# Attention scores as 64x64 products on the four quarters of the TensorE array, under a plan with other priorities

## Chip, cores and metric

One core of one Trainium2 chip. The metric is the device time of one execution in microseconds (us); lower is better. The kernel is one program: five engines, each with its own instruction queue in a fixed order, which wait for each other by semaphores.

## What is computed

Linear attention with decay in blocks, then two MLPs, all in float32. Cut to what matters here:

```python
# q, k, v: batch 2, 8 heads, 768 tokens, 64 wide
for b in range(nb):                                  # blocks of 64 tokens
    intra = einsum('bhic,bhjc->bhij', qb, kb) * Dmask   # scores, masked with lam ** (i - j)
    intra = einsum('bhij,bhjd->bhid', intra, vb)
    inter = einsum('bhid,bhde->bhie', qb * lam_pow, kv_state)
    out[:, :, sl] = intra + inter
    kv_state = lam_block * kv_state + einsum('bhsd,bhse->bhde', kb * rev_pow, vb)
x = heads side by side, (1536, 512)
h = x @ w_in;  x = (h * tanh(softplus(h))) @ w_out       # 512 -> 2048 -> 512
h = x @ w2_in; x = max(h, 0) ** 2 @ w2_out
```

## The kernel before

**Tiles and stages.** The kernel works on blocks of 128 tokens, twelve chunks, six per sequence. `attention(j)` (called for j = 0 to 5) records the operations of two chunks: load q and k (`qk`, transposed, so that the 64 columns of two heads lie on the 128 partitions) and k and v (`kv`); the scores `sc` (L514); their product with the mask on DVE, `a` (L371); the product of `a` with v into `xo` (L559, planned as av); q scaled in place on GpSimd (POOL, `qd`, L528) and k scaled in place (POOL, `kd`, L523); the update `sd` of the state, k times v (L540); the product of the scaled q with the state, added into the same `xo` (L568, "carried", planned as in); scaling (`ss`) and addition (`sa`) of the state on ACT, POOL and DVE; and copies of `xo` to SBUF on ACT and DVE (`xr`, `xh`, `xl`). Two MLPs follow. Each of their products is made as three products of rounded high and low parts (`mm3`, L380): `up`, `p`, `b`, `e`, `ua`, `ub` into the hidden layer, `dn`, `q`, `o`, `v` out of it, most of them by a scheme with seven products of blocks instead of eight. The weights come as 64-bit numbers that ACT (`m`, L658) and DVE (`t`, a shift of integers, L663, then a join L670) turn into float32, ACT and DVE then into high and low parts (`wh`, `wl`).

**Scores.** For each of four pairs of heads p and each head e of a pair, one product: 64 partitions (those of the head) of k, 128 columns, stationary, and 128 columns of q moving; the result takes 128 partitions of one bank of PSUM, bank e. Two products that follow each other use the lower and the upper 64 rows of the array. `carried` makes products of 64x64 stationary by 128 moving columns: 64 rows by head e, and 64 partitions of `xo` as output, so the four products that follow each other use the four quarters of the array.

```python
def weighted(p, e):                 # carried: which half of the output's partitions
    c = e if p < 2 else 1 - e
    return slice(c * D, (c + 1) * D)
for p in range(2):
    for e in range(2):
        for h in (p, p + 2):
            r = slice(e * D, (e + 1) * D)
            nc.tensor.matmul(out=o[weighted(h, e), h, n], lhsT=z[r, h], rhs=qd[r, h], ...)
```

**What sets the order.** Nothing above issues an instruction at once. Each call of `op(engine, us, fn, reads, writes, ...)` records an operation with an assumed duration; `Plan.run` then plays all of them by those durations and writes down the order in which each engine takes them, and that order is issued. PE takes its ready operation of lowest `rank` (which follows the order of the program); the others take the ready one that is due first. `Plan.dues` works the due times out backward from PE's, and the table `SOONER` shifts single ones by some microseconds. A DVE operation that only touches SBUF is lengthened in the plan by 0.8 (`SHARED`) of the time in which POOL works beside it. SP's queue issues all loads in planned order; the list `FIRST` fixes its first twelve.

Of the kernel before, what the change touches and what calls it, by code (L numbers as in the profile page):

```python
# [22 lines left out]
D = 64  # L23
# [10 lines left out]
SHARED = 0.8  # L34
# [69 lines left out]
class Op:  # L104
    def __init__(self, eng, us, fn, name, rank, lag, due, spare):
        self.eng, self.us, self.fn, self.name, self.rank = eng, us, fn, name, rank
        self.lag, self.due, self.spare = lag, due, spare
        self.before, self.after, self.vals = {}, {}, {}
        self.late, self.start, self.end = math.inf, None, None
        self.sooner = 0.0  # L110
        self.port = False


class Plan:
# [16 lines left out]
    def op(self, eng, us, fn, reads=(), writes=(), name="", rank=None, lag=None, due=None, spare=0, ahead=None, table=None, port=True):  # L131
# [17 lines left out]
        for v in o.vals:  # L149
            v.left += 1  # L150
        o.port = eng == "DVE" and port and all(v.space == "S" for v in o.vals)
# [163 lines left out]
def attention_mlps(ctx, tc, lam, qk, kv, w_in, w_out, w2_in, w2_out, out):  # L315
# [1102 lines left out]
    rank = 0  # L1418
# [111 lines left out]
```

## Time and profile before

| | before |
|---|---|
| median of three runs (lowest, highest) | 527.87 us (527.04, 529.77) |
| profiled execution: its time, its span | 527.82 us, 525.8 us |
| PE busy | 517.1 us, 98% of the span |
| DVE, ACT, POOL busy | 466.8, 429.3, 32.1 us |
| PE's share of the chain that ended last | 96% |
| DMA | 134.82 MB, 256 GB/s over the span |

The span is the profiled time from the first instruction to the last; the execution's own time holds some 2 us more around it. "Busy" counts the time in which an engine has an instruction under way; the rows of a matmul are passes, and a float32 product that is not split has two passes, so the 8 products of a chunk's scores are 16 rows of 64*128 (rows by columns of the stationary part). The start of the next row, not a row's duration, tells what a group of passes takes, since passes overlap.

### The profile page before, as it was taken

The page shows a single profiled execution, that of the slowest core. Times are in us where ns is not written, and L with a number is a line of the kernel's source. Part 1 is how long each engine was busy: PE and PEld are TensorE (multiplying, and loading weights), DVE is VectorE, ACT ScalarE, POOL GpSimd, SP SyncE. Part 2 cuts the span into 40 slices and gives each one's busy share as a digit, 9 for nine tenths or more (in the row PEclk, how much of TensorE's full clock was granted, in tenths as well). Part 3 has the DMA queues.
Part 4 walks back from the last instruction along what each step waited for, and adds up shares of the span by engine and source line. Part 5 has one row for each costly group of instructions (what it writes and reads, how often), then busy time and mean ns, then how long its engine had stood idle before and what let it go on. Part 6 is the DMA issues. An engine that isn't in the chain of part 4 may idle for free.

```text
span 525.8 us, 9377 instructions
## 1 busy us (share of the span) xinstructions
PE 517.1 (98%) x3686; PEld 464.6 (88%) x3686; DVE 466.8 (89%) x519; ACT 429.3 (82%) x506; POOL 32.1 (6%) x32
## 2 busy tenths in 40 slices
PE   7999999999999999999999999999999999999997
PEld 4898888898988989889888889998999889988996
DVE  6998998998996879998999999998999589995893
ACT  2859769889999999878999889869999689957852
POOL 2656200000000000000000000000000000000000
PEclk9999999999999999999999999999999999999999
DMA  8999812899479984996246897998289963891015
GB/s 300 410 408 347 342 37 84 272 340 407 181 283 364 320 233 129 347 401 246 80 150 240 351 359 258 336 365 267 78 290 359 347 205 123 303 413 43 1 46 195
DMA packets 39357, 134.82 MB, mean 256 GB/s; under 512 B 4242, under 2 KB 7314, under 8 KB 39314
## 3 DMA queue, kind: packets, MB, share of 16 engines
q1 hardware_dynamic: 39312, 134.23, 69.9%
q8 instruction: 29, 0.48, 0.3%
q14 instruction: 14, 0.11, 0.1%
q10 hardware_dynamic: 2, 0.00, 0.0%
HBM read 108.00 MB, written 26.21 MB: 255 GB/s over the span
## 4 chain that ended last, share of the span: by engine, by line
PE 96%; DVE 2%; DMA 1%; issue 0%; SPq 0%; DVEq 0%
PE p L380 17%; PE q L380 14%; PE v L380 11%; PE e L380 10%; PE o L380 10%; PE b L380 8%; PE ua L380 8%; PE ub L380 6%; PE dn L380 4%; PE up L380 2%; PE xo L559 2%; PE sc L514 2%; DMA st<-in_moe_w_in_dram 1%; PE xo L568 1%; PE sd L540 1%; DVE a L371 1%
## 5 line engine op out<-in xcount | busy, mean ns | idle before, releaser
L658 ACT ACTIVATE m<-st 128x512 f32<-128x512 f32 (+1 forms) x66 | 42.4, 671 | 12.1 <-DMA st<-in_moe_w_in_dram 8.2
L670 DVE SCALAR_TENSOR_TENSOR t<-m,t 128x1024 int32<-128x1024 int32 x32 | 39.4, 1250 | 3.9 <-ACT m L658 3.5
L371 DVE TENSOR_TENSOR sl<-s,sh 128x1024 fp32r<-128x1024 f32 x32 | 38.8, 1221 | 3.2 <-ACT sh L368 2.9
L371 DVE TENSOR_TENSOR wl<-t,wh 128x1024 fp32r<-128x1024 f32 x32 | 39.8, 1249 | 0.0
L371 DVE TENSOR_TENSOR el<-D,eh 128x1024 fp32r<-128x1024 f32 x32 | 38.8, 1219 | 0.8 <-ACT eh L368 0.8
L368 ACT ACTIVATE wh<-t 128x1024 fp32r<-128x1024 f32 x32 | 33.4, 1054 | 5.0 <-DVE t L670 4.8
L368 ACT ACTIVATE sh<-s 128x1024 fp32r<-128x1024 f32 x32 | 33.4, 1053 | 1.0 <-DVE s L371 1.0
L368 ACT ACTIVATE eh<-D 128x1024 fp32r<-128x1024 f32 x32 | 33.1, 1053 | 0.9 <-DVE D L371 0.9
L371 DVE TENSOR_TENSOR el<-h,eh 128x1024 fp32r<-128x1024 f32 x24 | 29.2, 1220 | 4.3 <-ACT eh L368 4.3
L663 DVE TENSOR_SCALAR t<-st 128x512 int32<-128x512 int32 (+1 forms) x66 | 27.3, 453 | 1.2 <-DMA st<-in_moe_w_in_dram 1.1
L368 ACT ACTIVATE eh<-h 128x1024 fp32r<-128x1024 f32 x24 | 25.2, 1056 | 0.3
L380 PE MATMUL p<-fl,wh 128*128 128x512 f32 x64 | 25.3, 395 | 0.0
L380 PE MATMUL p<-fh,wl 128*128 128x512 f32 x64 | 25.0, 391 | 0.0
L380 PE MATMUL p<-fh,wh 128*128 128x512 f32 x64 | 24.9, 389 | 0.0
L380 PE MATMUL p<-fl,sh 128*128 128x512 f32 x64 | 24.9, 389 | 0.0
L380 PE MATMUL p<-fh,sl 128*128 128x512 f32 x64 | 24.9, 389 | 0.0
L380 PE MATMUL e<-fl,sh 128*128 128x512 f32 x64 | 24.9, 389 | 0.0
L380 PE MATMUL e<-fh,sl 128*128 128x512 f32 x64 | 24.9, 389 | 0.0
L380 PE MATMUL p<-fh,sh 128*128 128x512 f32 x64 | 24.9, 389 | 0.0
L380 PE MATMUL e<-fh,sh 128*128 128x512 f32 x64 | 24.9, 389 | 0.0
L371 DVE TENSOR_TENSOR D<-h,h 128x1024 f32<-128x1024 f32 x16 | 18.9, 1220 | 2.1 <-ACT h L907 1.5
L368 ACT ACTIVATE ap<-o 128x1024 f32<-128x1024 f32 x18 | 18.4, 1022 | 2.8 <-PE o L380 2.6
(315 smaller groups left out, 1899.8 us busy)
## 6 DMA issues: line engine op xcount, KB each, us to landing
fh<-f SPq DMA_DIRECT2D x35, 512.0 KB, 5.7
fl<-f SPq DMA_DIRECT2D x35, 512.0 KB, 6.7
st<-in_moe_w_out_dram SPq DMA_DIRECT2D x32, 512.0 KB, 6.5
st<-in_moe_w_in_dram SPq DMA_DIRECT2D x26, 512.0 KB, 6.4
f<-fh SPq DMA_DIRECT2D x14, 512.0 KB, 6.0
f<-fl SPq DMA_DIRECT2D x14, 512.0 KB, 7.7
qk<-in_qk_dram SPq DMA_DIRECT2D x12, 512.0 KB, 10.2
kv<-in_kv_dram SPq DMA_DIRECT2D x12, 512.0 KB, 10.2
```

Of the source, the lines that this page charges most:

```text
L368: nc.scalar.activation(out=o, in_=i, func=AF.Copy)
L371: nc.vector.tensor_tensor(out=o, in0=a, in1=b, op=alu)
L380: nc.tensor.matmul(out=out_, lhsT=a, rhs=b, start=start, stop=pieces or (last and i == 2), skip_group_check=not start if pieces else onto)
L514: nc.tensor.matmul(out=o[:, e, p], lhsT=t[r, 1, p], rhs=t[r, 0, p], start=True, stop=True)
L540: nc.tensor.matmul(out=o[e * D : (e + 1) * D, p], lhsT=t[:, p, 1 + e], rhs=t[:, p, 0 if e else 3], start=True, stop=True)
L559: nc.tensor.matmul(out=o[weighted(p, e), p, n], lhsT=v[:, p, 0 if e else 3], rhs=w[:, e, p], start=p % 2 == n == 0, stop=True, skip_group_ ...
L568: nc.tensor.matmul(out=o[weighted(h, e), h, n], lhsT=z[r, h], rhs=qd[r, h], start=False, stop=True, skip_group_check=True)
L658: nc.scalar.activation(out=tl(m)[o, i], in_=tl(st, TB, 2)[r, :, 1].bitcast(F32), func=AF.Prelu, scale=RANGE, alpha=BELOW)
L663: nc.vector.tensor_scalar(out=tl(t)[o, i], in0=tl(st, TB, 2)[r, :, 0], scalar1=29, scalar2=None, op0=ALU.logical_shift_right)
L670: nc.vector.scalar_tensor_tensor(out=tl(t), in0=tl(m).bitcast(I32), scalar=3, in1=tl(t), op0=ALU.logical_shift_left, op1=ALU.bitwise_or)
```

## The change

Three edits. (1) `scores` splits each product by the columns of k: 16 products of 64x64 by 128 instead of 8 of 64x128 by 128; half 0 writes partitions 0 to 63 of the bank, half 1 partitions 64 to 127, so four products that follow each other use the four quarters. The planned durations become 1.6 and 0.88 us instead of 1.7 and 1.04. (2) The planner: the clocks of the engines start at 0.6 us and SP's at 1.1 instead of 0; the shift `t` of the weights gets `port=2`, with which a `t` that starts while POOL works is lengthened by all that POOL still has to do. (3) `SOONER` is another table, with 52 entries instead of 193. No load is changed: the same loads, with the same sizes; those behind the twelfth stand in another order.

```diff
 SOONER = {
-    "zero.1": -9.0, "lam.1": 28.5, "one.1": -1.5, "rate.1": 24.0, "eye.1": 4.5, "mask0.1": 24.0, "mask1.1": -1.5,
...
+    "eye.1": -1.5, "decay.1": 3.0, "qk0.1": -6.0, "kv0.1": 3.0, "kd0.1": 6.0, "kd1.1": 3.0, "ss1.1": 12.0,
...
@@
-        self.port = False
+        self.port = self.locks = False
@@
+        o.locks = port == 2
         o.port = eng == "DVE" and port and all(v.space == "S" for v in o.vals)
@@
-        clock = dict.fromkeys(self.LAG, 0.0)
+        clock = dict.fromkeys(self.LAG, 0.6)
+        clock["SP"] = 1.1
@@
                 if o.port and clock["POOL"] > now:
-                    o.end += SHARED * min(o.us, clock["POOL"] - now)
+                    o.end += clock["POOL"] - now if o.locks else SHARED * min(o.us, clock["POOL"] - now)
@@
                 t, o = tl(q, 2, NP, CH), tl(sc, 2, NP, CH)
                 for p in range(NP):
-                    for e in range(2):
-                        r = slice(e * D, (e + 1) * D)
-                        nc.tensor.matmul(out=o[:, e, p], lhsT=t[r, 1, p], rhs=t[r, 0, p], start=True, stop=True)
-
-            scored = op("PE", 1.7 if c < 2 else 1.04, scores, [(q, "q"), (q, "k")], [(sc, 0)], name=sc.name, rank=rank + n)
+                    for half in range(2):
+                        m = slice(half * D, (half + 1) * D)
+                        for e in range(2):
+                            r = slice(e * D, (e + 1) * D)
+                            nc.tensor.matmul(out=o[m, e, p], lhsT=t[r, 1, p, m], rhs=t[r, 0, p], start=True, stop=True)
+
+            scored = op("PE", 1.6 if c < 2 else 0.88, scores, [(q, "q"), (q, "k")], [(sc, 0)], name=sc.name, rank=rank + n)
@@
-            op("DVE", 0.34 * len(rows()), low, [(st, 0)], [(t, i)], name=f"t{name}{i}", spare=SPARE[1])
+            op("DVE", 0.34 * len(rows()), low, [(st, 0)], [(t, i)], name=f"t{name}{i}", spare=SPARE[1], port=2)
```

The new table moves instructions on every engine. In the rows below the number behind a name is that of its chunk or weight, and the one behind the underscore that of its buffer; xN is a count of products.

First place: PE, in the opening, from the product of chunk 1 with its masked scores (a1) on. Before:

```order
L559 MATMUL xo0_193<-a1_188,kv1_164 64x128 x8
L540 MATMUL sd0_218<-kv0_143 64x64 x8
L540 MATMUL sd0_218<-kv1_164 64x64 x8
L514 MATMUL sc2_244<-qk2_186 128x128 x8
L568 MATMUL xo0_193<-qk1_124,state0_255 64x128 x8
L514 MATMUL sc3_276<-qk3_204 128x128 x8
L559 MATMUL xo1_293<-a2_274,kv2_216 64x128 x8
L568 MATMUL xo1_293<-qk2_186,state0_255 64x128 x8
L540 MATMUL sd1_323<-kv2_216 64x64 x8
L380 MATMUL up0000_337<-xh00_285,wh0000_239 128x256
```

Now:

```order
L542 MATMUL xo0_208<-a1_200,kv1_172 64x128 x8
L551 MATMUL xo0_208<-qk1_124,state0_243 64x128 x8
L523 MATMUL sd0_223<-kv1_172 64x64 x8
L497 MATMUL sc2_275<-qk2_204 64x128 x16
L497 MATMUL sc3_305<-qk3_220 64x128 x16
L542 MATMUL xo1_330<-a2_303,kv2_241 64x128 x8
L551 MATMUL xo1_330<-qk2_204,state0_243 64x128 x8
L523 MATMUL sd1_358<-kv2_241 64x64 x8
L542 MATMUL xo1_330<-a3_326,kv3_292 64x128 x8
L551 MATMUL xo1_330<-qk3_220,state0_243 64x128 x8
L523 MATMUL sd1_358<-kv3_292 64x64 x8
L497 MATMUL sc4_410<-qk4_340 64x128 x16
```

The carried product of chunk 1 (xo0 from qk1 and state0) stands ahead of sc2 instead of behind it, sc2 and sc3 stand side by side, and sc4 with its load of qk4 stands ahead of all up products; before, up products stood between chunks 2 and 3, and the next scores behind them were those of chunk 7.

Second place: DVE, behind the masks and decay rows of the opening. Before:

```order
L663 TENSOR_SCALAR t0000_175<-st00000_136 128x512
L371 TENSOR_TENSOR a0_181<-sc0_149,mask_138 128x1024
L371 TENSOR_TENSOR a1_188<-sc1_166,mask_138 128x1024
L663 TENSOR_SCALAR t0000_175<-st00001_158 128x512
L670 SCALAR_TENSOR_TENSOR t0000_175<-m0000_177,t0000_175 128x1024
L371 TENSOR_TENSOR s0001_237<-t0000_175 128x512
L663 TENSOR_SCALAR t0001_241<-st00010_179 64x512 x2
L371 TENSOR_TENSOR wl0000_257<-t0000_175,wh0000_239 128x1024
L371 TENSOR_TENSOR a2_274<-sc2_244,mask_138 128x1024
L371 TENSOR_TENSOR state0_255<-sd0_218,state0_255 128x256
```

Now:

```order
L352 TENSOR_TENSOR a0_191<-sc0_153,mask_136 128x1024
L646 TENSOR_SCALAR t0000_197<-st00000_141 128x512
L352 TENSOR_TENSOR a1_200<-sc1_174,mask_136 128x1024
L646 TENSOR_SCALAR t0000_197<-st00001_170 128x512
L653 SCALAR_TENSOR_TENSOR t0000_197<-m0000_193,t0000_197 128x1024
L646 TENSOR_SCALAR t0001_267<-st00010_195 64x512 x2
L352 TENSOR_TENSOR state0_243<-sd0_223,state0_243 128x256
L352 TENSOR_TENSOR s0001_296<-t0000_197 128x512
L352 TENSOR_TENSOR a2_303<-sc2_275,mask_136 128x1024
L352 TENSOR_TENSOR a3_326<-sc3_305,mask_136 128x1024
L352 TENSOR_TENSOR xl00_353<-xo0_208,xh00_272 128x2x256
```

The masked scores a0 have changed places with the first shift t of a weight; a2 and a3 stand side by side behind the state's first addition, and wl0000 behind them.

Third place: PE between 42 and 50 us of the trace, the scores of chunks 6 to 9. Before:

```order
L514 MATMUL sc8_645<-qk8_455 128x128 x8
L514 MATMUL sc6_658<-qk6_578 128x128 x8
L540 MATMUL sd3_582<-kv7_553 64x64 x8
L514 MATMUL sc9_686<-qk9_319 128x128 x8
L540 MATMUL sd4_703<-kv8_344 64x64 x8
L540 MATMUL sd4_703<-kv9_427 64x64 x8
L559 MATMUL xo3_725<-a6_698,kv6_272 64x128 x8
L559 MATMUL xo3_725<-a7_474,kv7_553 64x128 x8
L568 MATMUL xo3_725<-qk7_290,state1_603 64x128 x8
```

Now:

```order
L551 MATMUL xo2_606<-qk5_356,state0_243 64x128 x8
L497 MATMUL sc6_660<-qk6_427 64x128 x16
L497 MATMUL sc7_679<-qk7_442 64x128 x16
L523 MATMUL sd3_704<-kv6_398 64x64 x8
L523 MATMUL sd3_704<-kv7_460 64x64 x8
L542 MATMUL xo3_729<-a6_698,kv6_398 64x128 x8
L542 MATMUL xo3_729<-a7_714,kv7_460 64x128 x8
L497 MATMUL sc8_755<-qk8_504 64x128 x16
L551 MATMUL xo3_729<-qk7_442,state1_753 64x128 x8
L497 MATMUL sc9_789<-qk9_534 64x128 x16
```

Scores and carried products (xo from qk and state) now stand side by side: that of chunk 5 with sc6 and sc7, that of chunk 7 between sc8 and sc9, and, further on, that of chunk 9 with sc10 and sc11. Before, scores and carried products were of two forms.

## Rows read from the trace of the kernel before

**Rows 1.** The page: busy time of PE; shares of the chain that ended last.
```profile
PE 517.1 (98%) x3686; PEld 464.6 (88%) x3686; DVE 466.8 (89%) x519; ACT 429.3 (82%) x506; POOL 32.1 (6%) x32
...
PE 96%; DVE 2%; DMA 1%; issue 0%; SPq 0%; DVEq 0%
```

**Rows 2.** Windows of the span: from:to length, then busy us (xinstructions) of the engines.
```profile
0.00:20.00 20.00, 15.28 (x182) 10.64 (x186) 15.33 (x26) 7.27 (x16) 7.76 (x13) 1.00 0.91 338
20.00:62.00 42.00, 41.88 (x652) 37.37 (x653) 38.34 (x44) 31.34 (x48) 24.37 (x20) 1.00 1.02 387
62.00:280.00 218.00, 218.00 (x1161) 188.99 (x1160) 198.44 (x219) 194.25 (x215) 0.00 (x0) 1.00 0.68 242
280.00:522.00 242.00, 241.89 (x1699) 227.62 (x1697) 214.32 (x234) 196.47 (x231) 0.00 (x0) 1.00 0.66 241
```

**Rows 3.** Timeline of PE, opening: start us, us, engine, line, operation, idle before.
```profile
8.36 1.04 PE L429 MATMUL warm<-zero 128*128 128x512 bf16 x4
11.28 1.09 PE L559 MATMUL xo<-a,kv 128*64 128x128 f32 x16 [1.87 <-DVE a L371]
12.78 1.09 PE L559 MATMUL xo<-a,kv 128*64 128x128 f32 x16 [0.41 <-DVE t L663]
...
15.34 1.16 PE L514 MATMUL sc<-qk 64*128 64x128 f32 x16 [0.54 <-DMA qk<-in_qk_dram]
16.43 0.67 PE L568 MATMUL xo<-qk,state 64*64 64x128 f32 x16
17.03 1.16 PE L514 MATMUL sc<-qk 64*128 64x128 f32 x16
18.90 1.09 PE L559 MATMUL xo<-a,kv 128*64 128x128 f32 x16 [0.71 <-DVE a L371]
19.93 0.67 PE L568 MATMUL xo<-qk,state 64*64 64x128 f32 x16
20.52 0.69 PE L540 MATMUL sd<-kv 128*64 128x64 f32 x16
```

**Rows 4.** Timeline of DVE and POOL in the same stretch.
```profile
8.53 1.27 POOL L528 TENSOR_TENSOR qk<-qk,misc 128x512 f32<-128x512 f32 x1 [6.98 <-PE sc L514]
...
8.81 1.28 DVE L663 TENSOR_SCALAR t<-st 128x512 int32<-128x512 int32 x1 [1.11 <-DMA st<-in_moe_w_in_dram]
10.01 2.34 DVE L371 TENSOR_TENSOR a<-sc,mask 128x1024 f32<-128x1024 f32 x2
...
10.16 1.06 POOL L523 TENSOR_TENSOR kv<-kv,mask 128x512 f32<-128x512 f32 x1 [0.36 <-DMA kv<-in_kv_dram]
...
12.27 0.41 DVE L663 TENSOR_SCALAR t<-st 128x512 int32<-128x512 int32 x1
...
12.71 1.06 POOL L523 TENSOR_TENSOR kv<-kv,mask 128x512 f32<-128x512 f32 x1 [1.49 <-DMA kv<-in_kv_dram]
```

**Rows 5.** Timeline of PE, 36 to 62 us.
```profile
36.40 2.06 PE L514 MATMUL sc<-qk 64*128 64x128 f32 x32
38.38 1.15 PE L540 MATMUL sd<-kv 128*64 128x64 f32 x32
...
53.00 2.54 PE L514 MATMUL sc<-qk 64*128 64x128 f32 x32
55.47 0.69 PE L540 MATMUL sd<-kv 128*64 128x64 f32 x16
...
59.57 1.10 PE L568 MATMUL xo<-qk,state 64*64 64x128 f32 x32
60.60 0.50 PE L380 MATMUL p<-fl,wh 128*128 128x512 f32 x1
...
62.10 0.39 PE L380 MATMUL dn<-gl,wh 128*128 128x512 f32 x1
```

**Rows 6.** Timeline of POOL: two multiplications that waited for a load.
```profile
25.51 1.42 POOL L523 TENSOR_TENSOR kv<-kv,mask 128x512 f32<-128x512 f32 x1 [0.57 <-DMA kv<-in_kv_dram]
...
34.50 1.06 POOL L523 TENSOR_TENSOR kv<-kv,mask 128x512 f32<-128x512 f32 x1 [2.29 <-DMA kv<-in_kv_dram]
```

41 rows, old and new, of the table SOONER are left out of this document.

## The prediction, made before the changed kernel ran

> **What bounds the kernel now.** I read the page first: TensorE is busy 98% of the span and 96% of the chain that ended last are its instructions [rows 1]. A share of busy time can hide waits, so the windows come next [rows 2]: from 20 us on PE is busy 41.88 of 42.00, 218.00 of 218.00 and 241.89 of 242.00 us, and the span ends at 525.8. So later DVE, ACT and DMA work is hidden, and the time can fall in two ways only: PE gets less to do, or it waits less before 20 us, where 4.7 us are not busy. It can rise through any new wait. Third, PE's timeline of the opening [rows 3] shows the waits one by one: 1.87 us before the product of chunk 0 with a0, 0.41 before chunk 1's, 0.54 before sc2 (a load), 0.71 before the product of chunk 2 with a2 (DVE). Fourth, the same microseconds on the other engines [rows 4] say what stands behind them. Fifth, PE's rows of 36 to 62 us give the prices of the product forms [rows 5]. The profiled execution took 527.82 us with a span of 525.8, that is 2.0 us around the span; the median of the three runs, 527.87, stands 0.05 above it, so the sum is made against 527.82 and read as the median.
>
> **Price of the scores.** A chunk's scores are now 8 products of 64x128 by 128, which the trace shows as 16 passes (x16, x32 for two chunks). Alone they take 1.09 us (15.34 to the next start at 16.43 [rows 3]), two chunks together 1.98 (36.40 to 38.38 [rows 5]); so the passes of a further chunk cost 0.89, and a start after another form costs 0.20. The new form is 16 products of 64x64 by 128, so 32 passes. No score runs in that form yet, but the carried products (L568) do: 64*64 against 64x128. Two of them, 32 passes, take 1.03 us (59.57 to 60.60 [rows 5]); one, 16 passes, takes 0.60 (16.43 to 17.03 [rows 3]). So 16 further passes cost 0.43, a start 0.17, and a chunk 1.03 alone, 0.87 when it follows another operation of the same form. Twice the passes at half the price each: the array gains almost nothing (0.87 against 0.89); what is gained are the starts, since scores and carried products now have the same form and can stand side by side.
>
> **The sum on PE from sc2 to the first dn product (62.10 [rows 5]).** I begin at sc2 because it waits for its load at 15.34 in both orders (below).
> - Scores of chunks 2 to 11 before: four alone, 4 x 1.09; two pairs, 2 x 1.98; the last pair 2.47 (53.00 to 55.47 [rows 5], so a stall of 0.49 within). Together 10.79. After: sc2 and sc3 side by side 1.03 + 0.87; sc4 and sc5 between up products 1.03 each; the other six stand beside carried products, 6 x 0.87. Together 9.18, a gain of 1.61. It counts the stall as gone; ends: 1.1 if the stall stays.
> - Carried product of chunk 1: it moves ahead of sc2 into time in which PE waits for the load. Gain 0.60; below, nothing, if state or POOL is late.
> - The wait of 0.71 for a2 goes as such (it is replaced, next point).
> - Other forms: the products are the same, and the runs of one form among them, each with one start, are 24 in either order (before: xo, sd and in in more runs at the front, fewer at the end). Nothing; a run more or less would be 0.17 to 0.20.
> Sum of the gains: 1.61 + 0.60 + 0.71 = 2.92.
>
> **What takes the place of the waits.** DVE: today the integer shift t takes 1.28 us at 8.81, against 0.41 at 12.27, because POOL multiplies qk1 from 8.53 to 9.80; a0 starts at 10.01 behind it, though its scores were done before 8.4 [rows 4]. In the change a0 stands ahead of t, right after the decay rows, so chunk 0's product (xo) no longer waits for DVE. But the next thing is late at once: kv0 lands at 10.16 and kv1 at 12.71, as POOL's waits show [rows 4], then qk2 at 15.34. The loads land one after another: kv0, kv1 and qk2 are the 4th, 6th and 8th that SP issues, and the 16th and 23rd (kv8, kv4) are waited for until 25.51 and 34.50 [rows 6], (34.50 - 25.51) / 7 = 1.28 us each. The first twelve loads are not moved. So the 1.87, 0.41 and 0.54 us turn into waits for kv0, kv1 and qk2, and nothing of them is gained but the place for the carried product.
> After sc2 comes the next such limit. The 13th and 14th load are now kv4 and qk4 (kv6 and qk7 before), and sc4 stands ahead of all up products on PE's queue, so everything behind it waits too. qk4 lands at 15.34 + 6 x 1.28 = 23.0. PE has before it sc2 and sc3 1.90, two xo at 1.03 (18.90 to 19.93 [rows 3]), two carried at 0.60 and two sd at about 0.6 (0.69 long with its last pass, 20.52 [rows 3]), less 0.17 where sd and xo stand in one run: 6.2 us, done at 21.5 if nothing else is late. That is a new wait of 1.47 us (estimate; 1.3 to 1.6 with slots of 1.27 to 1.30). Where it is shorter, a late chain has taken its place. Chains that this wait covers: a2 (scores done about 16.5, two of them then take DVE 2.34 us [rows 4]), the multiplications of qk2, kv2, qk3, kv3 on POOL at 1.06 to 1.27 each [rows 4] one after another, done about 22. Both may slip by about half a microsecond for nothing.
> The scores of chunks 0 and 1 and the four warm products behind them end at 9.4 [rows 3], 0.8 before kv0; they cost nothing unless they grow by more.
>
> **Sum:** 2.92 - 1.47 = 1.45 us less, 527.82 - 1.45 = 526.4. Behind dn PE's work is unchanged (two swaps of equal blocks), and I enter no wait there: the largest stretch shows PE full with DVE at 198.44 of 218.00 [rows 2], and the changes of DVE's and ACT's order behind 90 us are swaps of neighbours. The planner's other edits (the start of the clocks, the lock rule) emit no instruction; they act through the order, costed above.
>
> **The rivals.**
> - *Quarters in twos, slower.* If the new passes overlap two at a time, as the 64x128 ones do, and not four, a chunk costs 32 passes at 0.89/16, 1.78 us and a start: 0.91 to 0.95 more for each of chunks 4 to 11 and 1.86 for sc2 and sc3 together, 9.2 in all, of which the wait for qk4 swallows 1.5. Time 526.4 + 7.7 = 534.1. It decides as soon as 16 passes cost more than about 0.5. For it: the order of the quarters within a chunk is another than in L568 (rows of the array alternate first, there columns). Against: the 32 passes of L568 in 1.03 [rows 5] use the same four quarters and both banks. Chance 0.08. [...]
> - *DVE becomes the bound.* DVE has 42.00 - 38.34 = 3.7 us free between 20 and 62 us [rows 2]; with PE 1.5 us earlier, 2.2 remain. In the new order state additions stand ahead of ready work, so DVE may idle on sd. Beyond 2.2 us of new waits or POOL contention each microsecond delays dn; at 3.7 the gain is gone. Around 528 (527.4 to 529.4). Chance 0.18.
> - *The load is not late.* If qk4 comes a slot sooner, or chains keep PE busy until it, the wait of 1.5 goes: 524.9. Against: the even spacing of 1.28 from the 4th to the 23rd load. Chance 0.10.
> - *Starts do not merge*: the six scores cost 1.03 instead of 0.87, 527.4; that is the upper edge of my forecast.
>
> **How the numbers follow.** Forecast 526.4 with 525.4 to 527.4 around it, chance 0.60; the rivals 0.08, 0.18, 0.10; other mishaps (a late buffer for a load, a wait far behind) 0.04. What a measurement of this kernel can tell from no change is about 0.5%, 2.6 us: under 525.2 or over 530.5. Faster: most of the load rival and a little of the forecast's edge, 0.12. Slower: the twos, a bad case of DVE and the mishaps, 0.13. Same: 0.75. The range 524.8 to 529.2 holds the forecast, most of the load rival and most of DVE's, about 0.8.
>
> **What would show it.** Right: x32 score rows of 64*64 with starts 1.03 us apart alone, runs like sc-in-sc without a step between; the first xo near 10.2, PE waits for kv1, qk2 and above all for qk4 near 23.0; dn near 60.7; PE full from there, and the last product 1.5 us earlier. Wrong: scores of 1.9 us (first rival); PE waits behind DVE's a or wl between 37 and 63 us (second); sc4 before 22 us (third); any PE wait behind 90 us, which I priced at nothing.

## The result, and the profile after

The changed kernel takes 532.64 us (median of five runs, 532.3 to 533.08) against 527.17 for the kernel before (five runs in the same series): ratio 1.0093, interval 1.0075 to 1.0111. It is slower by about 5 us, and outside the range of 524.8 to 529.2. The profiled execution took 532.30 us with a span of 530.4.

The page and the windows first. The page of the changed kernel: busy time of PE, the queue that carries instructions, the chain.

```profile
PE 519.8 (98%) x3878; PEld 466.0 (88%) x3878; DVE 466.7 (88%) x519; ACT 427.6 (81%) x504; POOL 30.6 (6%) x32
...
q8 instruction: 31, 0.51, 0.4%
...
PE 94%; DMA 4%; issue 1%; SPq 0%; DVE 0%
```

Windows of the same kernel (columns as in [rows 2]; the last three are the granted clock, the DMA share and GB/s):

```profile
20.00:62.00 42.00, 38.15 (x693) 33.81 (x689) 33.88 (x39) 25.31 (x37) 22.92 (x20) 0.96 1.00 346
62.00:280.00 218.00, 218.00 (x1209) 188.84 (x1206) 198.59 (x218) 191.33 (x214) 0.00 (x0) 1.00 0.68 247
...
40.00:44.00 4.00, 4.00 (x124) 3.66 (x123) 4.00 (x6) 3.11 (x5) 0.63 (x1) 1.00 1.07 400
44.00:47.00 3.00, 3.00 (x77) 2.82 (x75) 2.73 (x4) 2.69 (x5) 1.63 (x2) 1.00 1.03 186
47.00:50.00 3.00, 0.67 (x21) 0.43 (x17) 2.76 (x3) 0.48 (x1) 1.48 (x2) 1.00 1.01 218
50.00:52.00 2.00, 2.00 (x44) 1.67 (x37) 0.24 (x1) 1.65 (x4) 0.62 (x1) 0.56 1.01 238
52.00:54.00 2.00, 2.00 (x40) 2.00 (x42) 1.28 (x2) 1.88 (x2) 1.28 (x1) 0.58 1.02 213
54.00:56.00 2.00, 2.00 (x44) 1.66 (x42) 1.50 (x2) 0.42 (x1) 0.59 (x1) 1.00 1.02 373
```

Where PE had 41.88 of 42.00 us from 20 to 62 [rows 2], it now has 38.15, and behind 62 it is full as before. So the loss lies ahead of the first dn product. The opening and the stretch of the hole on PE's timeline of the changed kernel:

```profile
14.81 1.10 PE L497 MATMUL sc<-qk 64*64 64x128 f32 x32 [0.58 <-DMA qk<-in_qk_dram]
16.66 1.10 PE L497 MATMUL sc<-qk 64*64 64x128 f32 x32 [0.74 <-DMA qk<-in_qk_dram]
...
23.05 0.88 PE L497 MATMUL sc<-qk 64*64 64x128 f32 x23 [0.24 <-DMA qk<-in_qk_dram]
24.35 0.54 PE L497 MATMUL sc<-qk 64*64 64x128 f32 x9 [0.42 <-issue]
...
30.76 1.10 PE L497 MATMUL sc<-qk 64*64 64x128 f32 x32
31.79 0.39 PE L361 MATMUL up<-xh,wh 128*128 128x256 f32 x1
...
41.33 1.93 PE L497 MATMUL sc<-qk 64*64 64x128 f32 x64
43.19 1.15 PE L523 MATMUL sd<-kv 128*64 128x64 f32 x32
...
46.02 1.10 PE L497 MATMUL sc<-qk 64*64 64x128 f32 x32
46.94 0.38 PE L551 MATMUL xo<-qk,state 64*64 64x128 f32 x2
49.65 0.55 PE L551 MATMUL xo<-qk,state 64*64 64x128 f32 x11 [2.33 <-issue]
...
50.04 1.90 PE L497 MATMUL sc<-qk 64*64 64x128 f32 x31
51.88 1.95 PE L523 MATMUL sd<-kv 128*64 128x64 f32 x32
53.64 1.06 PE L542 MATMUL xo<-a,kv 128*64 128x128 f32 x16
...
56.25 0.32 PE L551 MATMUL xo<-qk,state 64*64 64x128 f32 x1
57.19 0.56 PE L551 MATMUL xo<-qk,state 64*64 64x128 f32 x12 [0.62 <-issue]
...
66.46 0.39 PE L361 MATMUL dn<-gl,wh 128*128 128x512 f32 x1
```

The scores cost what was forecast: a chunk alone, 32 passes, takes 1.03 us to the next start (30.76 to 31.79), two chunks 1.86 (41.33 to 43.19). sc4 starts at 23.05, forecast 23.0. But then PE stops three times in the middle of an operation, with "issue" as the reason (it waited for nothing that the profile shows): within sc4, within the carried product of chunk 7 (in7 from here on) for 2.33 us, within that of chunk 9 (in9) for 0.62. Measured from start to start (0.69, 2.6 and 0.94) they make 4.2 us. Behind the second the granted clock is 0.56 and 0.58 for four microseconds (0.50 in a window from 50.25 to 53.66, 1.00 ahead of it and behind): the scores of chunk 9 take 1.84 to the next start instead of about 1.06, sd 1.76 instead of 0.98, another 1.6 us. The dn product comes at 66.46, forecast 60.7: 5.8 late, and 4.2 + 1.6 is 5.8.

What the stalls have in common is their count. The windows of the changed kernel, cut at the stalls:

```profile
0.00:24.30 24.30, 20.63 (x345) 14.69 (x345) 19.51 (x32) 13.98 (x29) 11.51 (x16) 1.00 0.94 361
24.30:49.00 24.70, 22.97 (x379) 21.25 (x380) 21.27 (x23) 12.90 (x16) 13.41 (x10) 1.00 1.03 365
49.00:57.10 8.10, 6.92 (x127) 5.88 (x126) 5.06 (x7) 4.59 (x6) 2.53 (x3) 0.79 1.01 281
```

PE and PEld together: 690 instructions ahead of the first stall, 759 up to the second, 253 up to the third, and 759 is 3 x 253. The page has 31 packets in the instruction queue for 7756 instructions of PE, 250 to a packet of 0.51/31 MB, 16 KB (the trace has 7911 records of TensorE with its semaphore instructions, 255 to a packet). (The experiments' expectations speak of 705, 1473 and 1729 records, 768 and 256 apart: all records of the trace, of which the windows' columns leave out some.) So each stall lies where one block of instructions ends. The kernel before has its 0.49 us within the scores at 53 us [rows 5] at the same place: 723 and 724, 1447 in all, ahead of 54.2. The DMA view of the changed kernel shows when a block came, here from 42.2 (a block's end by the count: 253 instructions ahead of the stall) to 46.9, then from 46.9 to 49.6:

```profile
q1 hardware_dynamic: 346, 1.21, 104.6%
...
q8 instruction: 1, 0.02, 2.8%
```

For 4.7 us there is no instruction packet, while the data queue fills all engines (104.6%); then there is one, and PE goes on at 49.65.

**Theory T**, then, worked out from these counts and packets: PE's instructions come in blocks of 256 (the 768 and 256 records between the stalls), and one block ahead is asked for when a block begins (my inference; no row shows the request). The packet waits behind data transfers (none for 4.7 us). With quarters a chunk's scores are twice as many instructions in about the same time, so a block is used up in 4.8 us (42.2 to 47.0, where the stall begins) and its successor isn't there. **Rivals:** the form itself or a hidden semaphore stalls these operations (Q); the new order and its transfers do it, not the form (O); moving transfers helps any kernel, whatever the instructions.

### The profile page after: what moved, and what is told of

Same layout as the page of the kernel before. It is cut to its first block, busy times and chain, and to the rows that moved or that the text cites. A ratio compares the mean times of both kernels' runs of the same rounds, so it can differ in the third digit from the quotient of the medians.

```text
span 530.4 us, 9776 instructions
## 1 busy us (share of the span) xinstructions
PE 519.8 (98%) x3878; PEld 466.0 (88%) x3878; DVE 466.7 (88%) x519; ACT 427.6 (81%) x504; POOL 30.6 (6%) x32
## 4 chain that ended last, share of the span: by engine, by line
PE 94%; DMA 4%; issue 1%; SPq 0%; DVE 0%
PE p L361 17%; PE q L361 14%; PE v L361 11%; PE e L361 10%; PE o L361 10%; PE b L361 8%; PE ua L361 8%; PE ub L361 6%; PE dn L361 4%; PE up L361 2%; DMA qk<-in_qk_dram 2%; PE sc L497 2%; DMA kv<-in_kv_dram 2%; PE xo L542 1%; PE xo L551 1%; PE sd L523 1%
```

## Experiments

**1. Form alone, order alone.** The first keeps the plan of before, the second takes the new plan without the new products.

```diff
# form only: the kernel before, with
+for half in range(2):
+    m = slice(half * D, (half + 1) * D)
     for e in range(2):
         r = slice(e * D, (e + 1) * D)
-        nc.tensor.matmul(out=o[:, e, p], lhsT=t[r, 1, p], rhs=t[r, 0, p], ...)
+        nc.tensor.matmul(out=o[m, e, p], lhsT=t[r, 1, p, m], rhs=t[r, 0, p], ...)
# order only: the changed kernel, with these lines as they were
```

> The kernel before with its own plan (order, priorities, loads) and only the scores written as four 64x64 products per pair of heads instead of two 64x128 ones. Theory T (TensorE's instructions are fetched in blocks of 256, one block ahead, by a transfer that waits behind the data transfers; the quarters double the score instructions, so a block is used up in under 6 us where its fetch can need over 7): stalls without any semaphore of 0.5 to 3 us each between 36 and 58 us, at multiples of 256 TensorE records from one another and not at the same operations as in the changed kernel; the long stalls in in7 and in9 move to other operations; 529 to 536 us. Rival O (the new order and its transfers do the harm, not the form): no stall over 0.5 us without a semaphore between 36 and 58 us, and about 526.5 us (score price less by 1.1 to 1.6 us, less what the old order can use of it).

> The changed kernel with its new plan and order, but the scores in the old form (two 64x128 products per pair of heads, half as many instructions). Theory T: a chunk takes 32 instructions fewer, so a block lasts 6 us and more as in the kernel before; stalls without a semaphore between 36 and 58 us add up to 0 to 1 us, the granted clock stays at 1.00 from 40 to 60 us, and the time is 527 to 529 us (the forecast of 526.4 plus the score gain of 1.1 to 1.6 us that is given up). Rival Q (the wait lies in a semaphore or a tile that the profile doesn't show, so it follows the order): in7 still stalls for over 1.5 us and in9 for about 0.6, 531 to 534 us. Rival O: the same as Q.

Form only: 533.11 us, 1.0104 (1.0087 to 1.012). Its timeline:

```profile
18.41 0.44 PE L516 MATMUL sc<-qk 64*64 64x128 f32 x6 [1.26 <-issue]
...
42.61 0.54 PE L570 MATMUL xo<-qk,state 64*64 64x128 f32 x10 [0.46 <-issue]
...
46.59 0.33 PE L542 MATMUL sd<-kv 128*64 128x64 f32 x3
50.51 1.72 PE L542 MATMUL sd<-kv 128*64 128x64 f32 x29 [3.59 <-issue]
51.92 3.05 PE L561 MATMUL xo<-a,kv 128*64 128x128 f32 x32
```

The old order stalls too, at other operations, even within an sd, which is no quarter product. Ahead of these stalls stand 440, 1197 and 1449 instructions: 757 and 252 apart, and 440 + 250 is the 690 of the changed kernel. Rival O, with 526.5, falls. Order only: 531.06 us, 1.006 (1.004 to 1.0081). The clock stays at 1.00 and in7 doesn't stall, against Q; one stall of 0.58 us lies within sc9, at count 1192:

```profile
49.44 1.05 PE L495 MATMUL sc<-qk 64*128 64x128 f32 x14 [0.58 <-issue]
```

I had expected 527 to 529. So the order costs 3 us and more by itself, and T in its first form did not say why; experiments 3 and 4 show a part of it.

**2. Shift.** Each of the four filling warm-up products becomes eight of 64 columns, 56 records more ahead of everything.

```diff
+def many_small():
+    z = zeros()
+    for i in range(8):
+        c = slice(64 * i, 64 * (i + 1))
+        nc.tensor.matmul(out=tl(warm)[:, 0, c], lhsT=z[:, 0:P], rhs=z[:, c], start=True, stop=True)
```

> The changed kernel in which each of the four filling warm-up operations behind the first scores is eight products of 64 columns instead of one of 512: the same columns, 28 instructions of each kind (weight load, product) more ahead of the first scan, so 56 records of TensorE more; nothing else. Theory T: the three stalls lie at the same counts of TensorE's records (705, 1473, 1729 on the trace of the changed kernel), so each comes 56 records earlier in the program: the long one out of in7 into the operations ahead of it (scores or half products of the chunks 6 to 8), that of in9 into what precedes it, that of sc4 to its beginning or ahead of it; total 531 to 535 us. Rivals: if the stall belongs to an operation (the quarter form itself, a tile, a hidden semaphore), in7 still stalls in its third pass and in9 in its second; same total.

534.74 us, 1.0136 (1.0116 to 1.0155). Timeline and windows of this run:

```profile
46.92 0.44 PE L504 MATMUL sc<-qk 64*64 64x128 f32 x7
49.85 1.60 PE L504 MATMUL sc<-qk 64*64 64x128 f32 x25 [2.48 <-issue]
...
55.68 0.43 PE L558 MATMUL xo<-qk,state 64*64 64x128 f32 x5
57.14 0.65 PE L558 MATMUL xo<-qk,state 64*64 64x128 f32 x11 [1.02 <-issue]
```

```profile
0.00:49.00 49.00, 42.80 (x725) 35.69 (x725) 38.30 (x53) 26.53 (x44) 24.42 (x25) 1.00 0.98 359
49.00:57.00 8.00, 6.27 (x126) 5.70 (x127) 4.59 (x6) 4.01 (x7) 3.15 (x3) 0.79 1.02 274
```

The long stall has left in7 and lies in the scores of chunk 8, behind the seventh pass; the other has left in9 for in8, 28 passes earlier. The count is unchanged: 1450, then 253. Q falls: the stall belongs to a count, not to an operation. That within sc4 vanished instead of moving; no row says why. Of the 2 us above the changed kernel, 1.5 lie in the opening (sc4 starts at 24.60 instead of 23.05).

**3. The same order, transfers out of the way.** The loads of the weight tiles st010.. (the second group of w_in; two of the four, st01010 and st01011, come as two transfers of 64 rows each) and the stores o0x (the high and low parts of the attention's output, put away in DRAM) go behind the store o0t00 on SP's queue; PE's order stays. Then the same with the old score form.

```diff
-op("SP", 1.3, load, [], [(st, 0)], ...)
+op("SP", 1.3, load, [], [(st, 0)], ..., ahead=30.0 if (L, g, kind) == (0, 1, 0) else None)
-op("SP", 1.3, ..., name=f"aw{L}{kind}{n}{m}")
+op("SP", 1.3, ..., name=f"aw{L}{kind}{n}{m}", ahead=16.0 if L == 0 and kind == "x" else None)
```

> The changed kernel with its order on TensorE untouched, in which the loads of the weight tiles st010.. and the stores of the o0x outputs are issued behind the store o0t00, some 10 us later, so that the data transfers between 46 and 58 us are gone or few. Theory T: the instruction block asked for at the boundary near 42 to 47 us is fetched at once instead of up to 4.9 us later; the stall of 2.6 us in in7 shrinks to under 0.8 us, that in in9 to under 0.3 us, the granted clock stays at 1.00 from 49 to 54 us, dn comes near 62 us, and the time is 526.5 to 529 us (later loads of the weight tiles may cost up to 1 us of it). The stall in sc4 near 24 us stays. Rivals (form, order or a hidden semaphore): in7 and in9 stall as before, 531 to 534 us.

> The changed kernel's order with the scores in the old form (64x128) and with the loads of st010.. and the stores of o0x issued later, as in the quiet variant of the changed kernel (528.03 us). Theory T: with the fetches on time the two differ by the price of the score form alone. From the rows of the traces: ten chunks behind the opening take 10.33 us of TensorE in quarters (quiet variant) and 11.4 in halves (with the new order), so this one takes about 1.1 us longer, 529.1 (528.6 to 529.7), with no stall without a semaphore between 40 and 58 us. Rival F (the quarters gain nothing even then): 528.0, equal. Rival Q (hidden wait in the new order): a stall in in7 as in the run with the order alone (0.6 and 0.5 us), 530 to 531.

Quarters: 528.03 us, 1.0003 (0.9993 to 1.0013), 4.6 us less than the changed kernel. Windows and timeline:

```profile
44.00:47.00 3.00, 3.00 (x80) 2.83 (x76) 3.00 (x5) 2.99 (x5) 1.64 (x2) 1.00 0.30 117
47.00:50.00 3.00, 2.87 (x90) 2.45 (x84) 2.78 (x4) 1.93 (x5) 2.85 (x4) 1.00 0.03 8
50.00:52.00 2.00, 2.00 (x46) 1.66 (x44) 1.83 (x3) 1.94 (x3) 0.74 (x2) 1.00 0.00 0
```

```profile
24.43 0.54 PE L498 MATMUL sc<-qk 64*64 64x128 f32 x9 [0.16 <-issue]
...
47.03 1.06 PE L552 MATMUL xo<-qk,state 64*64 64x128 f32 x13
...
61.87 0.39 PE L362 MATMUL dn<-gl,wh 128*128 128x512 f32 x1
```

No stall is listed in in7 or in9 any more (0.13 of the 3 us from 47 to 50 are still idle), the clock stays at 1.00, dn comes at 61.87. Halves: 527.78, 0.9997 (0.9986 to 1.0007); I expected 529.1, and my claim that the quarters are worth 1.1 us falls. From the start of sc4 to dn both take 38.49 us (quarters 23.38 to 61.87, halves 23.22 to 61.71). Pairs of score groups cost 1.86 instead of 1.99 and two carried products ahead of them 0.12 less each, together the forecast's 0.24 a pair; but the quarters still lose 0.16 and a restart of some 0.3 within sc4, and about 0.2 within in7 (13 passes in 0.8 to the next start, where 16 take 0.60). Gain and loss cancel.

**4. Which transfers, and why.** The stores alone later; the loads alone later; the loads where they were, but as one transfer of 128 rows (the halves of these tiles' rows then stand in the other order, so the run shows the cause and is no cure as it stands).

```diff
# straight: the two tiles st01010, st01011
-if turned and g:        # two transfers of 64 rows, halves exchanged
+if turned and g > 1:
```

> The changed kernel with only the four stores o0x later; the loads of st010.. stay where they were (issued at 37 to 44 us). Theory T: the fetch that is late for in7 is asked for at 42.2 and starts at 46.96, ahead of nearly all of the stores (46.75 to 51.72), so it waits behind the loads: in7 still stalls by 1.5 to 2.7 us and the clock falls behind it; the next fetch, asked for about 49.6, finds no stores, so the stall of 0.6 in in9 goes: 530 to 532 us. Rival S (the stores are what is in the way): in7 doesn't stall, 527.5 to 529.

> The complement of the run with the stores later: the changed kernel with only the loads of st010.. later (behind the store o0t00), the four stores o0x where they were, at about 47 to 52 us. Theory T: the fetch asked for at 42.2 finds the transfer engines free from about 44 us on and starts by 45.5, so in7 doesn't stall (under 0.4 us) and the clock stays at 1.00; the next ones, asked for at about 47.5 and 52.5, can meet the stores; if the stores fill the engines as the loads did, a stall of 0.3 to 2 us comes near 52 to 57 us, if not, none. 527.5 to 530 us. Rival S (any transfer of this volume does it, loads or stores alike; or the stall belongs to in7): in7 stalls by 1.5 us or more, 530.5 to 532.5.

> The changed kernel in which the two tiles st01010 and st01011 are loaded as one transfer of 128 rows each instead of two of 64 rows with the halves exchanged, at the same place of the queue; so these two blocks of the first layer's weights have their halves of rows in the other order, and the products with them are not those of the reference. Everything else as in the changed kernel. What is asked: why the transfer engines are full at half their rate from 44 to 54 us, so that the fetch waits behind them. Theory T, first form (the transfers into 64 rows at a time move at half rate): packets take about 0.16 us all through 44 to 54 us instead of 0.3, the transfers run at about 400 GB/s and are done before 50 us, the fetch asked for at 42.2 starts by 46, in7 stalls by under 0.8 us, the clock stays at 1.00: 527.5 to 529.5 us. Second form (these loads are slow whatever the rows, by where they read in the weights): 200 GB/s from 44 to 54 us as before, the stall in in7 stays at 2 us and more, 531.5 to 533.5 us.

Stores later: 531.8 us, 1.0064 (1.0041 to 1.0088). in7 stalls by 2.04, in9 by 0.88, which I had expected to go: the loads alone hold the engines at 213 to 240 GB/s and a share of about 1 up to 52 us.

```profile
49.96 0.55 PE L551 MATMUL xo<-qk,state 64*64 64x128 f32 x11 [2.04 <-issue]
```

Loads later: 527.61, 0.9999 (0.999 to 1.0008), no such stall; the stores alone do no harm. Its window, then windows and timeline of the straight loads (528.95 us, 1.0028, 1.0014 to 1.0042):

```profile
44.00:47.00 3.00, 3.00 (x76) 2.72 (x76) 3.00 (x5) 2.97 (x6) 1.65 (x2) 1.00 1.02 410
```

```profile
44.00:47.00 3.00, 3.00 (x82) 2.81 (x78) 3.00 (x5) 2.99 (x5) 1.63 (x2) 1.00 1.03 406
47.00:50.00 3.00, 2.60 (x82) 2.19 (x75) 2.32 (x4) 1.68 (x4) 3.00 (x4) 1.00 1.03 408
50.00:52.00 2.00, 2.00 (x51) 1.66 (x48) 2.00 (x3) 2.00 (x3) 0.80 (x1) 1.00 1.05 422
```

```profile
47.85 0.55 PE L551 MATMUL xo<-qk,state 64*64 64x128 f32 x11 [0.40 <-issue]
...
54.07 0.55 PE L551 MATMUL xo<-qk,state 64*64 64x128 f32 x12 [0.85 <-issue]
```

So it is the two loads in pieces of 64 rows. With them the engines are full (1.01 to 1.03) at 186 to 238 GB/s from 44 to 54 us; with 128 rows they are full at 406 to 422 up to 52 us, and the stall in in7 falls from 2.33 to 0.40, with no fall of the clock. Why a transfer into 64 rows gets half the rate is not shown. A stall of 0.4 us in in7 and one of 0.85 in in9 (more than the 0.62 of the changed kernel) stay even at full rate: the quarters still use up a block faster than the next one comes.

**5. Can either kernel be beaten?** The old order with later transfers, with quarters, with halves, and with halves for the first chunks only; and the same mixture in the new order.

```diff
# old order, later: the edit of experiment 3, with 16.0 for the loads and all eight stores of L == 0
# mixed, old order (new order: 6 for 4)
-for half in range(2):
-    m = slice(half * D, (half + 1) * D)
+for half in range(2 if c >= 4 else 1):
+    m = slice(half * D, (half + 1) * D) if c >= 4 else slice(0, P)
```

> The kernel before with its own order on TensorE, the scores in quarters, and the loads of st010.. and the stores of o0x and o0t issued later. The candidate to beat both kernels. Theory T: the stalls of 0.5 and 3.6 us of the run with the form alone go (under 0.5 us in all between 36 and 58 us) and the clock stays at 1.00; the scores give 1 us and the stall of 0.4 us of the kernel before goes too: 526 to 527.5 us. The stall of 1.3 us in sc3 near 18 us is not touched by the edit and may stay. Rival O (form and old order don't go together whatever the transfers do): 530 to 533.

> The kernel before, scores in halves, with the same later loads and stores as the previous one; the control for it. Theory T: its only late fetch is the one of 0.4 us at 54 us, so it gains 0 to 0.5 us: 527.2 to 527.9. If moving transfers were a gain by itself, whatever the instructions (rival: contention of the transfers with the engines), it would gain the 4 us and more that the changed kernel gained from it: 523 to 525.

> The kernel before with its own order, the later loads and stores (527.33 us with scores in halves, 528.68 with quarters), and quarters for the chunks 4 to 11 only, halves for 0 to 3: 128 records of TensorE fewer in the opening, where the all-quarters version stalled by 1.13 us at sc3. Theory T: that stall goes, as the block that contains it lasts longer than its fetch needs; the blocks of 36 to 58 us still last 4 to 6 us, so a few tenths of stall may stay at the boundaries there; the quarters gain about 0.25 to 0.6 us in their joins against the halves: 526.7 to 527.7 us. Rival: the stall at sc3 was not the fetch but a late landing that the profile doesn't name; then PE waits there as long with the halves too, and it is 528 to 529.

> The quiet variant of the changed kernel (528.03 us) with halves for the chunks 0 to 5 and quarters for 6 to 11: 192 records fewer ahead of the first run of quarters. Theory T: the small stall within sc4 near 24 us (0.16 us and a restart of 0.3) goes, since no boundary lies in scores there any more; the rest as in the quiet variant, 527.2 to 527.9 us. Rival: the form costs or gains nothing anywhere and 528.0 is the order's own time: 527.9 to 528.2.

The kernel before took 527.17 us in the series of the result and 527.65 to 527.86 in those of the experiments, so the medians of different series are compared by their ratios.

| scores, transfers | old order | new order |
|---|---|---|
| halves, as planned | 527.17 (before) | 531.06 |
| quarters, as planned | 533.11 | 532.64 (after) |
| halves, later | 527.33, 0.9984 (0.9973 to 0.9995) | 527.78 |
| quarters, later | 528.68, 1.0011 (1.0 to 1.0022) | 528.03 |
| mixed, later | 527.2, 0.9994 (0.9984 to 1.0004) | 527.61, 0.9997 (0.9988 to 1.0006) |

The control (halves, old order, later) gained 0.8 us by its ratio, a little more than the 0 to 0.5 that I gave it, far from the 4.6 of the changed kernel: moving the transfers helps where blocks run out. In its timeline the stall of 0.49 us at 53 us is gone (1.99 to the next start, 54.94, instead of 2.47):

```profile
52.95 2.06 PE L514 MATMUL sc<-qk 64*128 64x128 f32 x32
```

It is the one version that beats both kernels, by less than the 0.5% that the prediction took for what a measurement can tell. Quarters in the old order missed the 526 to 527.5 expected: stalls of 1.13, 0.55 and 0.30 us stay at counts 441, 1198 and 1450, the first in the opening, where the edit moved nothing. With halves there (mixed) that stall is gone, and 0.33 us at one later boundary is left. In the new order the mixture has no stall in sc4, and takes 38.08 us from sc4 to dn, against 38.49 for both pure forms: the quarters' own gain, where they don't stall, is 0.4 us by these profiles; the medians (527.61 and 527.78) don't tell it from noise.

## Why the prediction was wrong

- **Right:** the form's price (the rival of quarters in twos, 1.78 us a chunk, didn't happen: 32 passes take 1.03 us); the carried product of chunk 1 ahead of sc2; all waits of the opening turned into waits for loads; sc4 released by qk4 at 23.05 (forecast 23.0). The wait shown at sc4 is 0.24 instead of 1.47, as 0.74 for qk3 and 0.18 and 0.25 for kv stand ahead of it; together the place is the same. The rivals of DVE and of a load that isn't late fell with it. (In three variants of this order chunk 1's product with a1 does wait for DVE's t, by 0.77, 0.77 and 2.14 us.)
- **The step that failed** is the sum from sc4 to dn, 23.0 to 60.7, 37.7 us; it was 43.41 (23.05 to 66.46). "Price of the scores" doubled the passes and priced their time on the array, and entered nothing for bringing twice the instructions. The 192 instructions more of each kind (3686 to 3878) were given pass time only, and the one sign in the trace of before, the stall of 0.49 us within the scores at 53 us [rows 5], was entered as a gain ("It counts the stall as gone; ends: 1.1 if the stall stays."), without asking what it was. It was the same wait, at the same count (it went with the later transfers, experiment 5), and the change made it larger: 4.2 us of stalls, and 1.6 us of low clock behind the longest.
- **The order was not free either.** I looked at what the new order of loads does to the opening, and not at 37 to 44 us, where it issues the loads in pieces of 64 rows in two pairs, at 37.44 and 42.69, with two whole tiles between; the kernel before issues all four pieces one behind the other from 40.49. From 44 to 54 us the engines then move half as much (186 to 238 GB/s); in the kernel before only 46 to 50 us (234 to 258 GB/s) are like that. Why the same pieces are slow for twice as long isn't shown. With halves this costs 3 us (531.06 against 527.78 with later transfers). Of it the trace shows 0.6 and a restart of 0.3 as a stall and 0.53 as a wait of sd for state; some of the rest may be the load of qk4: sc4 starts between 23.05 and 24.60 in the profiles of this order. The remainder isn't placed.
- **Mis-sized:** the gain of 1.61. Ten chunks of scores took 10.33 us in the quiet variant against 10.79 before, a gain of 0.46, with the stall at 53 us gone: sc2 and sc3 are kept apart by the wait for qk3 (0.3), sc4 has its restart (0.3), sc8 and sc9 are split by in7 (0.3), the last pairs' second starts are saved in the carried products instead. Behind dn the new order takes 463.9 to 464.2 us (463.6 with the straight loads), the old 463.7 to 463.8: a loss of 0.2 to 0.4 where I had entered nothing.

That one block is asked for ahead is worked out from the counts and the packets; no row shows the request itself. The start times of the instruction packets in the traces bear it out. From 80 us on, where PE doesn't stop, a packet of the changed kernel starts every 256 TensorE records on the mean (5641 records for 22 packets). And each stall named above ends 2.3 to 2.8 us after such a packet's start (46.96 to 49.65, 54.59 to 57.19), 3.2 for the longest, in the run with the form only; so a packet that starts without a stall brings a later block than the one in use.

## What to carry to other kernels

Count instructions as well as their time on the array: where a change doubles the number of products, divide the time of the busiest stretch by the blocks of instructions it uses up, and compare that with how long a block takes to come beside the data transfers there (42.2 to 49.65 us, 7.4, in the changed kernel; 5.5 and 6.2 us at full transfer rate, with the straight loads). An idle time with no releaser in the middle of one operation, at a fixed count of instructions, is the sign, and it is worth chasing in the trace of before, however small. The cure is in the transfers: one of 128 rows instead of two of 64 took 3.7 us off the changed kernel, later ones 4.6, without touching the engine that waited.

## What was not expected of the hardware

- Instruction blocks queue behind data: in the changed kernel 4.7 us without a packet (42.2 to 46.9) while the data queue takes 104.6% of the engines, then 2.7 us from the packet's start to the next pass. In the quiet variant the data queue takes 53.0% in the same window, one packet comes within it, and in7 doesn't stall. The late blocks of these runs cost stalls of 0.16 (quiet variant, sc4) to 3.59 us (form only, sd).
- Transfers into 64 rows fill all engines at half the rate: 186 to 238 GB/s at a share of 1.01 to 1.03 (changed kernel, 44 to 54 us) against 406 to 422 at 1.03 to 1.05 (straight loads, 44 to 52 us).
- After stalls of 2.0 to 3.6 us the granted clock fell to 0.50 to 0.68 for some four microseconds (four runs, windows 50 to 52 and 52 to 54 us: changed kernel 0.56 and 0.58, form only 0.68 and 0.50, shift 0.51 and 0.64, stores later 0.62 and 0.53); after stalls of up to 1.3 us it stayed at 1.00 (form only, 1.26 us in sc3, window 18 to 20), and so it did after a wait of 2.14 us in the opening of the shift run (window 0 to 20), so the length of the stop alone doesn't decide it.
- The first scores run slowly or fast from run to run of like code: 64 quarter passes take 3.69 us in the changed kernel, 2.29 in the run with the form only. The windows print a clock of 1.00 for both, but the clock records of the traces begin only at 9.29 and 6.34 us, at the full level, and the passes speed up at that moment (kernel before, record from 7.21 us: a pair of passes every 0.21 us up to 7.1, every 0.11 from 7.3 on). In all eight kernels that start with these 64 passes the time follows that record (2.26 us where it begins at 6.29, 2.97 at 7.74, 3.69 at 9.24 to 9.52). So it is most likely the clock's rise, not the code.
